# Attention into a mixture-of-depths layer: the hand-written order of 1162 items drawn anew

## The chip, the cores and the metric

The kernel runs on one core of a Trainium2 chip. The metric is device time in microseconds, from launch to end, the median of several runs. The engines of the core run side by side, each in its own order: PE (TensorE, matmuls), DVE (VectorE), ACT (ScalarE), POOL (GpSimd, which here mostly issues DMAs) and SP (SyncE, which only issues DMAs). An engine waits for another on semaphores.

## What is computed

Eight batches, twelve heads, 448 tokens, 64 columns per head. First attention with a squared ReLU, then for each batch a router picks 128 of the 448 tokens and a two-layer expert is added to them alone.

```python
scores = scale * np.matmul(q, k.transpose(0, 1, 3, 2))
attn = np.maximum(scores, 0.0) ** 2 / S
out = np.matmul(attn, v)                      # then heads side by side: x [8, 448, 768]

scores = np.einsum('bsd,d->bs', x, w_gate)
for b in range(B):
    top_idx = np.argpartition(-scores[b], capacity)[:capacity]      # capacity 128
    xe = x[b, top_idx]
    ye = np.maximum(xe @ w1, 0.0) @ w2                               # 768 -> 1024 -> 768
    g = 1.0 / (1.0 + np.exp(-scores[b, top_idx]))
    out[b, top_idx] = x[b, top_idx] + g[:, None] * ye
```

## The kernel before

The attention is cut into 24 units of four heads, three to a batch (unit u belongs to batch u // 3). For each unit, in the words of the order:

- `L,q,u`, `L,k,u`, `L,v,u` load the unit from memory (POOL's queue, cast to bf16 on the way). There are six buffers of each, so a load for unit u waits for the last reader of unit u - 6. Units 15 to 20 are loaded in two halves.
- `T,u,0` and `T,u,1` transpose q and k on PE (14 matmuls against an identity each, tile shape 128x64). `TE,u,2` copies both out of PSUM to `qkt` (DVE).
- `S,u,c` (c from 0 to 6) is a score block: four matmuls of tile shape 64x64 that run side by side. `R,u,c` is its ReLU, out of PSUM to `r_sb` (all on ACT). `Q,u,0,3` and `Q,u,3,7` square three and four of these blocks on DVE (`a_sb` from `r_sb`, twice the same input).
- `V,u,c` is the product with v (four 64x64 matmuls). `X,u` takes the unit's result out of PSUM to `xT_sb`, on ACT or DVE, as the letter A or D says.
- For units outside `BYDMA`'s batches `RT,u` transposes that back to rows on PE, and `RE,u` copies them to `x_rows`. For batches 5 and 6 `XB,u` does it with two transposing DMAs on SP's queue. `ST,b` stores a batch's rows (two DMAs on POOL's queue).

For each batch b the expert follows. `colx` and `colE` make the router's scores, `bt`, `rk`, `cs0`, `cs`, `rank` and `hots` rank the tokens, `sel,b` and `sE,b` give the 128 indices (`idx`, the last a reduction on DVE). `XG,b` gathers these rows from memory into `xg` (an indirect DMA on POOL's queue; it also needs the batch's `ST` to have landed). `XT,b` transposes them on PE, `xeE` copies them out, `gs` and `sig` make the sigmoid. `h,b,f` (f from 0 to 7) is the first layer, six matmuls of shape 128x128 each, `hE` its ReLU; `y,b,f` is the second layer, two matmuls of 384 columns, `yE` takes it to `gye` times the sigmoid, and `ADD,b` adds it to memory (an indirect DMA on POOL's queue). Batch 7, the last, takes its rows by matmuls (`xe`) instead of a gather. `W,i,part` loads parts of the weights. `PW,n,bank` are n matmuls on zeros that only keep PE busy at the start. `Zx`, `Zg`, `Zw` and the like are set-up: `Zh` copies the identity to fp32, `Zg` transposes the gate weights on PE, `Zc` makes constants.

A single string, ORDER, lists all these items, and a loop issues them as they stand. So it alone sets the order on every engine and queue: each engine takes its items in the string's order. The numbers at an item's end name a PSUM bank. There are eight banks, and an item that writes one waits for the last reader of what stood in it.

```python
with tc.manual_schedule():
    for item in ORDER.split():
        name, *args = item.split(",")
```

Transposes have a second form. A switch in their argument list does each in two halves of 64 columns, which gives them the tile shape 128x64 in place of 128x128:

```python
for h in HALF if by64 else (slice(0, 128),):
    nc.tensor.matmul(out=out_[h], lhsT=in_[:, h], rhs=ident, is_transpose=True,
                     skip_group_check=True, **flags)
```

Of the kernel before, what the change touches and what calls it, by code (L numbers as in the profile page):

```python
# [21 lines left out]
def kernel(  # L22
# [22 lines left out]
    BYDMA = (5,6)  # L45
# [60 lines left out]
    def L(what, u):  # L106
# [3 lines left out]
        if b not in BYDMA:  # L110
            nc.gpsimd.dma_start(out=dst, in_=src(t, u))  # L111
            return
# [224 lines left out]
    class Moe:  # L337
# [11 lines left out]

        def g(self, i, bank=None):  # L350
            if i == 0:
                self.at["g"] = bank
            nc.tensor.matmul(out=PS[:, self.at["g"], :S],
                             lhsT=wg_col[:, 1, i:i + 1].to_broadcast([128, 128]), rhs=self.xT[:, i].rearrange("p c n -> p (c n)")[:, :S],
                             start=(i == 0), stop=(i == NM - 1), skip_group_check=True)

        def colx(self, u, bank=None):
            if u == 0:
                self.at["col"] = bank
            for m in (2 * u, 2 * u + 1):  # L360
                for c in range(NR):
                    nc.tensor.matmul(out=PS[:, self.at["col"], c:c + 1], lhsT=self.xT[:, m, c, :],  # L362
                                     rhs=wg_col[:, 1 - (self.b in BYDMA), m:m + 1],
# [114 lines left out]
        def h(self, f, bank=None):  # L478
            if f == 0:
                self.at["h"] = bank  # L480
            bk, o = divmod(f * 128, 512)
            for m in range(NM):
                nc.tensor.matmul(out=PS[:, self.at["h"] + bk, o:o + 128],  # L483
                                 lhsT=w1_sb[:, m, f * 128:(f + 1) * 128], rhs=self.xeT[:, m, :],
                                 start=(m == 0), stop=(m == NM - 1), skip_group_check=True)
# [64 lines left out]
    R,7,2,A W,1,6,8 L,q,10 RT,3,0,1 rk,1,1 W,0,2,6 S,7,3,6 R,8,1,A RE,3,D rk,1,3 R,8,2,A Q,7,0,3 V,6,0,2 V,6,1  # L550
    V,6,2 W,0,3,6 L,k,11 R,7,3,A V,6,3 V,6,4 S,7,4,4 R,7,4,A S,7,5,0 T,10,0,6 T,10,1 XG,0 S,7,6,4 TE,10,2,D
    V,6,5 R,7,5,A R,7,6,A V,6,6 X,6,A cs0,1,0 cs,1,0 cs,1,1 cs,1,2 rank,1 hots,1 W,1,2,8 XT,0,0,1 S,8,3,4
    S,8,4,6 R,8,3,A R,8,4,A xeE,0,2,D sel,1,0 sE,1 S,8,5,2 W,0,1,6 h,0,0,0 h,0,1 h,0,2 R,8,5,A S,8,6,4 S,9,0,6
# [117 lines left out]
```

## Time and profile before

| | |
|---|---|
| runs, us | 198.83, 200.74, 202.49 (median 200.74) |
| the profiled execution, us | 199.68, of it the span 197.9 |
| mean granted TensorE clock | 0.987 |
| PE, DVE, ACT, POOL busy, us | 179.1, 164.7, 162.5, 109.2 |
| HBM traffic over the span | 284 GB/s |

The span runs from the first to the last instruction. What the launch takes beside it is 1.8 us. A busy share is an average over stages with different limits, so it says where to look and not what a change is worth; that is read in the stage itself, from what ends a wait there last.

### The profile page before, as it was taken

The numbers are of one execution on the slowest core, as the hardware profiler recorded it, in microseconds if no ns is written. First come the engines' busy times: TensorE is split into PE (matmuls) and PEld (weight loads), VectorE is DVE, ScalarE is ACT, GpSimd is POOL, SyncE is SP. The second block draws the span as 40 slices with busy tenths as digits, with TensorE's granted clock in tenths as the row PEclk, the third lists the DMA queues.
The fourth block names the chain that finished last, engine by engine and source line by source line (L and its number), as shares of the span: only waits on it lengthen the run. The fifth ranks groups of instructions, "written<-read, shape, count | busy, mean of one in ns | idle before, by whom it ended". The sixth has DMA issues, their size and how long they took to land.

```text
span 197.9 us, 7244 instructions
## 1 busy us (share of the span) xinstructions
PE 179.1 (91%) x3186; PEld 124.1 (63%) x3186; DVE 164.7 (83%) x234; ACT 162.5 (82%) x204; POOL 109.2 (55%) x160
## 2 busy tenths in 40 slices
PE   7778898989899999999998999999999999999900
PEld 7455455657567675875776767776676466688600
DVE  2489999999989999999999899999997999753310
ACT  4689999999999998999998999899998997242300
POOL 7968654641863967758897694460203140853360
PEclk9999999999999999999999999999999999999995
DMA  5999999999999999999999999999557892199291
GB/s 175 140 184 203 203 205 205 235 322 206 201 248 298 203 182 200 202 195 283 177 152 172 344 205 288 262 145 170 226 106 106 92 311 55 18 251 240 55 135 24
DMA packets 32333, 37.70 MB, mean 191 GB/s; under 512 B 8744, under 2 KB 29614, under 8 KB 31278
## 3 DMA queue, kind: packets, MB, share of 16 engines
q0 software_dynamic: 24928, 34.74, 91.1%
q1 hardware_dynamic: 7374, 2.50, 8.8%
q8 instruction: 25, 0.41, 0.8%
q14 instruction: 6, 0.05, 0.1%
HBM read 42.08 MB, written 14.16 MB: 284 GB/s over the span
## 4 chain that ended last, share of the span: by engine, by line
PE 56%; ACT 17%; DMA 11%; POOL 7%; issue 4%; DVE 2%; POOLq 0%; DVEq 0%
ACT r_sb L216 15%; PE ps L260 12%; PE ps L483 10%; PE ps L499 9%; PE ps L281 7%; PE ps L233 5%; DMA q_sb<-in_q_dram 4%; DMA v_sb<-in_v_dram 4%; PE ps L295 4%; POOL out_dram L517 3%; DMA xg<-out_dram,idx 3%; PE ps L209 2%; PE ps L374 2%; PE ps L362 2%; POOL k_sb L111 1%
## 5 line engine op out<-in xcount | busy, mean ns | idle before, releaser
L216 ACT ACTIVATE r_sb<-ps 128x896 bf16<-128x896 f32 x168 | 140.8, 955 | 8.1 <-PE ps L260 7.1
L274 DVE TENSOR_TENSOR a_sb<-r_sb 128x2688 bf16<-128x2688 bf16 (+1 forms) x48 | 84.9, 1785 | 2.4 <-ACT r_sb L216 2.0
L260 PE MATMUL ps<-qkt 64*64 64x448 bf16 x672 | 55.6, 362 | 4.3 <-ACT r_sb L216 2.5
L281 PE MATMUL ps<-a_sb,v_sb 64*64 64x448 bf16 x672 | 42.1, 351 | 0.8 <-ACT r_sb L216 0.8
L260 PEld LDWEIGHTS <-qkt 64*64 64x64 bf16 x672 | 21.4, 104 | 21.7 <-issue 11.4
L220 DVE COPY qkt<-ps 128x1792 bf16<-128x1792 bf16 (+3 forms) x26 | 26.1, 1006 | 4.4 <-PE ps L233 2.8
L281 PEld LDWEIGHTS <-v_sb 64*64 64x64 bf16 x672 | 21.5, 106 | 9.5 <-issue 2.2
L443 POOL DMA_INDIRECT xg<-out_dram,idx x7 | 12.2, 1748 | 27.4 <-DVE idx L427 23.6
L499 PE MATMUL ps<-w_sb,hT 128*128 128x384 bf16 x128 | 25.2, 326 | 0.0
L483 PE MATMUL ps<-xeT,w_sb 128*128 128x128 bf16 x384 | 24.5, 219 | 0.2 <-DVE xeT L220 0.2
L483 PEld LDWEIGHTS <-w_sb 128*128 128x128 bf16 x384 | 21.8, 98 | 4.5 <-issue 4.2
L517 POOL DMA_INDIRECT out_dram<-gye,idx x9 | 15.7, 1741 | 9.5 <-ACT g__3725 L476 5.9
L216 ACT ACTIVATE xT_sb<-ps 128x896 bf16<-128x896 f32 x16 | 15.4, 963 | 3.0 <-PE ps L281 2.9
L111 POOL DMA_DIRECT2D v_sb<-in_v_dram x18 | 13.2, 731 | 6.5 <-PE ps L281 2.8
L327 POOL DMA_DIRECT2D out_dram<-x_rows x8 | 4.5, 567 | 21.9 <-DMA x_rows<-xT_sb 13.6
L233 PEld LDWEIGHTS <-q_sb 128*64 128x64 bf16 x336 | 11.2, 111 | 6.5 <-issue 5.5
L233 PE MATMUL ps<-ident,q_sb 128*64 128x128 bf16 x336 | 14.1, 223 | 1.1 <-ACT r_sb L216 0.6
L499 PEld LDWEIGHTS <-hT 128*128 128x128 bf16 x128 | 10.6, 97 | 7.2 <-issue 2.2
L111 POOL DMA_DIRECT2D q_sb<-in_q_dram x17 | 12.7, 749 | 4.0 <-PE ps L233 1.5
L111 POOL DMA_DIRECT2D k_sb<-in_k_dram x17 | 12.5, 736 | 3.5 <-PE ps L260 1.5
L233 PE MATMUL ps<-ident,k_sb 128*64 128x128 bf16 x336 | 13.9, 220 | 0.0
L385 DVE SCALAR_TENSOR_TENSOR mask_sb<-ps,cols,tie 128x448 bf16<-128x448 f32 (+2 forms) x24 | 12.3, 546 | 0.7 <-PE ps L374 0.6
(123 smaller groups left out, 196.7 us busy)
## 6 DMA issues: line engine op xcount, KB each, us to landing
out_dram<-x_rows POOLq DMA_DIRECT2D x8, 768.0 KB
out_dram<-x_rows POOLq DMA_DIRECT2D x8, 576.0 KB, 7.3
v_sb<-in_v_dram POOLq DMA_DIRECT2D x18, 224.0 KB, 6.5
q_sb<-in_q_dram POOLq DMA_DIRECT2D x17, 224.0 KB
k_sb<-in_k_dram POOLq DMA_DIRECT2D x17, 224.0 KB, 8.3
w_sb<-in_moe_w_dram POOLq DMA_DIRECT2D x6, 256.0 KB
w_sb<-in_moe_w_dram POOLq DMA_DIRECT2D x8, 192.0 KB
k_sb<-in_k_dram POOLq DMA_DIRECT2D x12, 112.0 KB, 4.6
```

The source lines that it names most:

```text
L111: nc.gpsimd.dma_start(out=dst, in_=src(t, u))
L216: nc.scalar.activation(out=out_, in_=in_, func=func or AF.Copy, scale=scale)
L220: nc.vector.tensor_copy(out=out_, in_=in_)
L233: nc.tensor.matmul(out=PSB[HALF[j], at["T", u, w], n * 128:(n + 1) * 128], lhsT=s[:, j, c, :], rhs=ident, is_transpose=True, start=(n == 0 ...
L260: nc.tensor.matmul(out=PS[HALF[hf], bank + j, :S], lhsT=qkt[u][HALF[j], 1, c, hf, :], rhs=qkt[u][HALF[j], 0, :, hf, :], start=True, stop=True)
L274: nc.vector.tensor_tensor(out=a_sb[u][:, c0:c1], in0=r, in1=r, op=ALU.mult)
L281: nc.tensor.matmul(out=PS[HALF[j], at["V", u] + hf, :S], lhsT=v_sb[u % NBUF][HALF[hf], j, c, :], rhs=a_sb[u][HALF[hf], c, j, :], start=(c ...
L385: nc.vector.scalar_tensor_tensor(out=mask, in0=row[:, o:S], scalar=self.cols[:, c:c + 1], in1=tie[:, :S - o], op0=ALU.subtract, op1=ALU.is ...
L443: read = reads[self.b] = nc.gpsimd.indirect_dma_start(out=self.xg, out_offset=None, in_=out[0:self.b + 1].rearrange("b s d -> (b s) d"), i ...
L483: nc.tensor.matmul(out=PS[:, self.at["h"] + bk, o:o + 128], lhsT=w1_sb[:, m, f * 128:(f + 1) * 128], rhs=self.xeT[:, m, :], start=(m == 0) ...
L499: nc.tensor.matmul(out=PS[:, self.at["y"] + w, :384], lhsT=self.hT[:, f, :], rhs=w2_sb[:, f, w * 384:(w + 1) * 384], start=(f == 0), stop= ...
L517: add = nc.gpsimd.indirect_dma_start(out=out[0:self.b + 1].rearrange("b s (w d) -> (b s w) d", w=w), out_offset=bass.IndirectOffsetOnAxis( ...
```

## The change

The list of items that go by transposing DMAs now names units and no longer batches; it names the same six. Two items get a new argument: `h` and `y` can be done in halves of 64 columns, as transposes could. And the ORDER string is replaced by another of the same 1162 items.

```diff
-    BYDMA = (5,6)
+    BYDMA = (15,16,17,18,19,20)
...
-        if b not in BYDMA:
+        if u not in BYDMA:
...
+        def order(self, m):
+            return 1 - (NU * self.b + m // 2 in BYDMA)
...
-        def h(self, f, bank=None):
+        def h(self, f, by64, bank=None):
...
-        def y(self, f, part, bank=None):
+        def y(self, f, part, by64, bank=None):
             if bank is not None:
                 self.at["y"] = bank
             for w in ((0,), (1,), (0, 1))[part]:
-                nc.tensor.matmul(out=PS[:, self.at["y"] + w, :384], lhsT=self.hT[:, f, :],
-                                 rhs=w2_sb[:, f, w * 384:(w + 1) * 384], start=(f == 0),
-                                 stop=(f == NF - 1), skip_group_check=True)
+                for p in HALF if by64 else (slice(0, 128),):
+                    nc.tensor.matmul(out=PS[p, self.at["y"] + w, :384], lhsT=self.hT[:, f, p],
+                                     rhs=w2_sb[:, f, w * 384:(w + 1) * 384], start=(f == 0),
+                                     stop=(f == NF - 1), skip_group_check=True)
...
     ORDER = """
-    S,0,4,6 S,0,5,4 R,0,2,A R,0,3,A R,0,4,A R,0,5,A S,0,6,0 R,0,6,A Q,0,0,3 T,1,0,2 L,k,1 T,1,1 TE,1,2,D Lw Zg,4
-    Zw PW,15,5 S,1,0,0 S,1,1,2 R,1,0,A L,q,2 Q,0,3,7 L,k,2 T,2,0,4 T,2,1 S,1,2,6 S,1,3,0 R,1,1,A R,1,2,A R,1,3,A
...
+    Zx,1 R,0,2,A S,0,3,2 R,0,3,A Q,0,0,3 S,0,4,6 R,0,4,A S,0,5,4 S,0,6,0 R,0,5,A Zh T,1,0,2 T,1,1 TE,1,2,D
+    PW,19,6 S,1,0,2 T,2,0,4 R,0,6,A S,1,1,0 T,2,1 R,1,0,A R,1,1,A L,v,0 L,k,3 S,1,2,2 Zx,0 Q,0,3,7 V,0,0,6
```

The halves of `y` are asked for in five items (`y,1,0` to `y,1,2`, `y,4,6`, `y,4,7`), those of `h` in none. `RT` is done in halves in none (before: units 10 and 12), `XT` in batches 2, 3 and 5 (before: 3 alone). The engine letter differs in some evictions: `RE` of units 7, 9, 10, 22, 23, `X` of 9 and 20, `hE,7,1`, `xeE,1`, `xeE,7,1`, `yE,4`, `yE,7,0`, and the first two copies of `qkt`. `PW` has 62 matmuls before and 66 now.

Three places of the order follow. A name ends in a number that tells buffers apart; between the two kernels these numbers need not agree.

On DVE, at the start: the copy of unit 1's `qkt` with its neighbours, two squares (L274) of unit 0 and what stands between. Before:

```order
L274 TENSOR_TENSOR a_sb_283<-r_sb_237 128x2688
L220 COPY qkt_314<-ps_84 128x1792
L198 CAST wg_col_110<-ps_84 128x12
L274 TENSOR_TENSOR a_sb_283<-r_sb_237 128x3584
L220 COPY qkt_394<-ps_84 128x1792
L274 TENSOR_TENSOR a_sb_422<-r_sb_345 128x2688
```

The same place now:

```order
L274 TENSOR_TENSOR a_sb_271<-r_sb_261 128x2688
L187 CAST ident_f_119<-ident_118 128x128
L220 COPY qkt_316<-ps_84 128x1792
L274 TENSOR_TENSOR a_sb_271<-r_sb_261 128x3584
L220 COPY qkt_410<-ps_84 128x1792
L274 TENSOR_TENSOR a_sb_415<-r_sb_374 128x2688
```

The copy of the gate weights (`wg_col`) is gone from here, and the copy of the identity has come in ahead of `qkt`; it stood third on DVE before.

On POOL's queue, from batch 2's store (L327, L328) to batch 2's gather (`xg` with `idx`): loads of units 17 to 19, and one or two scatters (`gye`). Before:

```order
L327 DMA out_0_dram<-x_rows_1590 64x3072
L328 DMA out_0_dram<-x_rows_1590 64x2304
L115 DMA q_sb0_85<-in_q_dram 64x2x448 x2
L115 DMA q_sb4_89<-in_q_dram 64x2x448 x2
L517 DMA out_0_dram<-gye_2057,idx_1124 896x768
L115 DMA q_sb1_86<-in_q_dram 64x2x448 x2
L443 DMA xg_2339<-out_0_dram,idx_1580 128x768
L115 DMA v_sb0_97<-in_v_dram 64x2x448 x2
```

The same place now:

```order
L327 DMA out_0_dram<-x_rows_1612 64x3072
L328 DMA out_0_dram<-x_rows_1612 64x2304
L111 DMA v_sb1_98<-in_v_dram 128x2x448
L115 DMA q_sb5_90<-in_q_dram 64x2x448 x2
L115 DMA k_sb0_91<-in_k_dram 64x2x448 x2
L523 DMA out_0_dram<-gye_1694,idx_700 448x768
L115 DMA k_sb3_94<-in_k_dram 64x2x448 x2
L446 DMA xg_2237<-out_0_dram,idx_1591 128x768
L115 DMA q_sb3_88<-in_q_dram 64x2x448 x2
```

Between store and gather stands batch 0's scatter (448 rows down) where batch 1's stood (896), and behind the gather stands the q load of unit 15 (`q_sb3`) where the v load of unit 18 stood (`v_sb0`).

On DVE, around the reduction that gives batch 3's indices (`idx_2130` in both). Before:

```order
L274 TENSOR_TENSOR a_sb_2474<-r_sb_2357 128x2688
L220 COPY qkt_2534<-ps_84 128x1792
L427 TENSOR_REDUCE idx_2130<-ps_84 128x1
L220 COPY x_rows_2248<-ps_84 128x4x256
L368 TENSOR_TENSOR cols_2520<-ps_84,skew_106 128x4
L274 TENSOR_TENSOR a_sb_2474<-r_sb_2357 128x3584
```

The same place now:

```order
L220 COPY qkt_2557<-ps_84 128x1792
L371 TENSOR_TENSOR cols_2568<-ps_84,skew_106 128x4
L430 TENSOR_REDUCE idx_2130<-ps_84 128x1
L274 TENSOR_TENSOR a_sb_2487<-r_sb_2351 128x3584
L220 COPY x_rows_2182<-ps_84 128x4x256
```

A square now stands directly behind the reduction; before, a copy of rows and the scores of batch 4 stood between them.

## Rows read from the trace of the kernel before

**Rows 1.** The page, part 1: busy us, share of the span, instructions.

```profile
PE 179.1 (91%) x3186; PEld 124.1 (63%) x3186; DVE 164.7 (83%) x234; ACT 162.5 (82%) x204; POOL 109.2 (55%) x160
```

**Rows 2.** Windows: length, PE, PEld, DVE, ACT, POOL busy, clock, DMA share, GB/s.

```profile
13.00:51.00 38.00, 34.55 (x671) 21.79 (x668) 37.16 (x39) 36.78 (x46) 21.24 (x34) 1.00 1.22 223
51.00:188.00 137.00, 134.59 (x2382) 94.64 (x2378) 120.48 (x174) 117.28 (x148) 73.83 (x98) 1.00 0.99 192
```

**Rows 3.** Timeline, PE, 61 to 67 us: start, length, line, tile shape, count.

```profile
61.83 1.18 PE L483 MATMUL ps<-xeT,w_sb 128*128 128x128 bf16 x18
62.94 0.38 PE L260 MATMUL ps<-qkt 64*64 64x448 bf16 x4
63.26 0.84 PE L483 MATMUL ps<-xeT,w_sb 128*128 128x128 bf16 x12
64.03 0.38 PE L260 MATMUL ps<-qkt 64*64 64x448 bf16 x4
...
66.33 0.38 PE L260 MATMUL ps<-qkt 64*64 64x448 bf16 x4
66.52 0.38 PE L281 MATMUL ps<-a_sb,v_sb 64*64 64x448 bf16 x4
```

**Rows 4.** Timeline, all engines, 11 to 14 us; in brackets idle time before.

```profile
11.68 1.09 DVE L220 COPY qkt<-ps 128x1792 bf16<-128x1792 bf16 x1 [0.35 <-PE ps L233]
...
12.44 1.01 PE L209 MATMUL ps<-zero 128*128 128x128 bf16 x15
...
13.38 0.57 PE L260 MATMUL ps<-qkt 64*64 64x448 bf16 x8
...
13.82 0.92 ACT L216 ACTIVATE r_sb<-ps 128x896 bf16<-128x896 f32 x1 [0.85 <-PE ps L260]
```

**Rows 5.** Timeline, POOL, 88 to 100 us: store, scatter and gather among loads.

```profile
88.43 1.19 POOL L115 DMA_DIRECT2D k_sb<-in_k_dram  x2 [2.37 <-PE ps L281]
89.61 0.54 POOL L327 DMA_DIRECT2D out_dram<-x_rows  x1
...
90.69 2.40 POOL L115 DMA_DIRECT2D q_sb<-in_q_dram  x4
94.57 2.81 POOL L517 DMA_INDIRECT out_dram<-gye,idx  x1 [1.48 <-DVE gye L222]
...
98.99 1.61 POOL L443 DMA_INDIRECT xg<-out_dram,idx  x1 [0.30 <-issue]
```

**Rows 6.** Timeline, PE: unit 15's transposes (L233), gathers' (L295), a selection (L422).

```profile
101.29 0.56 PE L233 MATMUL ps<-ident,q_sb 128*64 128x128 bf16 x14
...
104.61 0.51 PE L295 MATMUL ps<-ident,xg 128*128 128x128 bf16 x6 [0.57 <-DMA xg<-out_dram,idx]
...
113.33 0.27 PE L422 MATMUL ps<-tok,hot__2129 128*128 128x2 bf16 x4
...
123.28 0.50 PE L295 MATMUL ps<-ident,xg 128*64 128x128 bf16 x12
```

**Rows 7.** Timeline, DVE and POOL: squares and gathers, 126 to 150 us.

```profile
126.82 1.55 DVE L274 TENSOR_TENSOR a_sb<-r_sb 128x2688 bf16<-128x2688 bf16 x1
...
128.36 2.02 DVE L274 TENSOR_TENSOR a_sb<-r_sb 128x3584 bf16<-128x3584 bf16 x1
128.72 2.54 POOL L443 DMA_INDIRECT xg<-out_dram,idx  x1 [2.79 <-DVE idx L427]
...
149.19 0.98 POOL L443 DMA_INDIRECT xg<-out_dram,idx  x1 [8.52 <-DVE idx L427]
```

**Rows 8.** Chain of work that ended last: start, length, what.

```profile
39.96 8.85 DMA q_sb<-in_q_dram
```

**Rows 9.** Timeline, PE and POOL, 185 us to the end.

```profile
185.38 1.62 PE L499 MATMUL ps<-w_sb,hT 128*128 128x384 bf16 x9
...
188.10 1.56 POOL L517 DMA_INDIRECT out_dram<-gye,idx  x1 [0.52 <-ACT gye L216]
...
189.96 1.55 POOL L517 DMA_INDIRECT out_dram<-gye,idx  x1 [0.26 <-issue]
```

More of the change, by code (lines that the diff above doesn't have):

```diff
@@ L353, in g @@
             nc.tensor.matmul(out=PS[:, self.at["g"], :S],
-                             lhsT=wg_col[:, 1, i:i + 1].to_broadcast([128, 128]), rhs=self.xT[:, i].rearrange("p c n -> p (c n)")[:, :S],
+                             lhsT=wg_col[:, self.order(i), i:i + 1].to_broadcast([128, 128]), rhs=self.xT[:, i].rearrange("p c n -> p (c n)")[:, :S],
                              start=(i == 0), stop=(i == NM - 1), skip_group_check=True)
@@ L362, in colx @@
                     nc.tensor.matmul(out=PS[:, self.at["col"], c:c + 1], lhsT=self.xT[:, m, c, :],
-                                     rhs=wg_col[:, 1 - (self.b in BYDMA), m:m + 1],
+                                     rhs=wg_col[:, self.order(m), m:m + 1],
                                      start=(m == 0 and c == 0),
@@ L482, in h @@
             for m in range(NM):
-                nc.tensor.matmul(out=PS[:, self.at["h"] + bk, o:o + 128],
-                                 lhsT=w1_sb[:, m, f * 128:(f + 1) * 128], rhs=self.xeT[:, m, :],
-                                 start=(m == 0), stop=(m == NM - 1), skip_group_check=True)
+                for p in HALF if by64 else (slice(0, 128),):
+                    nc.tensor.matmul(out=PS[p, self.at["h"] + bk, o:o + 128],
+                                     lhsT=w1_sb[:, m, f * 128 + p.start:f * 128 + p.stop],
+                                     rhs=self.xeT[:, m, :], start=(m == 0), stop=(m == NM - 1),
+                                     skip_group_check=True)
         def hE(self, part, eng):
@@ L550 @@
[L550 to L553, printed above, removed]
-    h,0,3 h,0,4 Q,7,3,7 h,0,5 S,9,1,2 h,0,6 Q,8,0,3 h,0,7 R,8,6,A S,9,2,4 R,9,0,A Q,8,3,7 V,7,0,6 V,7,1 L,v,8
@@ L610 @@
[L610 to L614 removed]
+    Zz LFq Cq,0 Zi Zs PW,32,0 LFk,0,2 Cq,1 Ck,0,2,D LFk,2,7 Zt Zm T,0,0,0 Zc L,q,1 TQE,0,4,D TK,0,2 TKE,0,2,D
@@ new lines @@
+    T,19,0,2 T,19,1 TE,19,2,D S,17,4,6 V,16,0,0 V,16,1 R,18,0,A V,16,2 S,17,5,4 L,v,18 hots,4 V,16,3 V,16,4
+    V,16,5 V,16,6 R,17,4,A R,17,5,A X,16,D XB,16 S,17,6,2 R,17,6,A h,3,0,0,6 sel,4,4 h,3,1,0 h,3,2,0 sE,4
+    S,18,1,0 S,18,2,2 S,18,3,4 h,3,3,0 h,3,4,0 h,3,5,0 h,3,6,0 h,3,7,0 R,18,1,A R,18,2,A R,18,3,A S,18,4,0
+    Q,17,0,3 XG,4 V,17,0,2 Q,17,3,7 V,17,1 R,18,4,A S,19,0,4 R,19,0,A V,17,2 V,17,3 V,17,4 V,17,5 hE,3,2,D
+    S,19,1,0 R,19,1,A V,17,6 X,17,D S,19,2,6 R,19,2,A T,20,0,4 T,20,1 TE,20,2,D S,18,5,0 XB,15 colx,5,0,2
@@ new lines @@
+    colx,5,1 colx,5,2 colE,5 R,18,5,A S,19,3,6 S,19,4,4 S,18,6,0 Q,18,0,3 R,19,3,A R,19,4,A R,18,6,A bt,5,2
+    gs,3,3 rk,5,2 rk,5,0 y,3,0,2,0,6 rk,5,3 y,3,1,2,0 y,3,2,2,0 sig,3 rk,5,1 y,3,3,2,0 y,3,4,2,0 S,19,5,0
+    S,19,6,4 Q,18,3,7 R,19,5,A cs0,5,3 XT,4,0,2 cs,5,0 R,19,6,A L,k,23 cs,5,1 cs,5,2 y,3,5,2,0 y,3,6,2,0
+    y,3,7,2,0 rank,5 yE,3,2,D xeE,4,2,A S,20,0,0 T,21,0,4 T,21,1 S,20,1,2 S,20,2,6 R,20,0,A R,20,1,A V,18,0,0
+    V,18,1 V,18,2 V,18,3 V,18,4 hots,5 TE,21,2,D V,18,5 L,v,21 S,20,3,2 S,20,4,4 V,18,6 R,20,2,A Q,19,0,3
@@ L615 @@
+    y,7,6,1,0 y,7,7,1,0 sel,7,3 sig,7 yE,7,1,A sE,7 ADD,6 y,7,1,0,0 y,7,2,0,0 y,7,3,0,0 y,7,4,0,0 y,7,5,0,0
+    y,7,6,0,0 y,7,7,0,0 yE,7,0,A ADD,7,1 ADD,7,0
     """
```

152 lines of the change are left out of this document (74 added, 78 removed).

## The prediction

> **What bounds the kernel now.** I read the page's busy shares first: TensorE (PE) is busy 91% of the span, and VectorE (DVE) and ScalarE (ACT) stand close behind at 83% and 82% [rows 1]. With three engines so near each other the mean says little, so I read the stages. The table of windows has two [rows 2]. From 13 to 51 us DVE works 37.16 and ACT 36.78 of 38 us, and PE idles 3.45: the evictions set the pace. From 51 to 188 us PE works 134.59 of 137 us, so it idles 2.4 us, while ACT has 19.7 us to spare and DVE 16.5: PE sets the pace, to the last matmul. The granted clock is 1.00 in both, the 2.4 GHz level. Behind the last matmul (188.2 us) come two scatters from POOL, the last issued at 189.96 [rows 9], and the span ends at 197.9: a tail of 9.7 us. So only three things can move the time: ACT's start and its holes before 51 us, PE's own work and holes after it, and the tail.
>
> I then went through PE's rows one piece of the order at a time. A piece of the same kind always takes the same time from its start to the next start, except where the shape of the tile in use changes. The four matmuls of a score block are followed after 0.19 us by value matmuls of the same 64x64 shape (66.33 to 66.52), but after 0.32 us by 128x128 matmuls (62.94 to 63.26): that change costs 0.13. The other way, 18 matmuls of the expert's first layer take 1.11 us up to a score block (61.83 to 62.94) and 12 take 0.77 (63.26 to 64.03), so six take 0.34 and the change of shape 0.10 [rows 3]. I take 0.11 for a change in either direction. Where I speak of PE work between two places below, it is the sum of such pieces over the order, waits left out.
>
> **The change, part by part.** The code of the two new arguments and of the renamed list computes what it did: the same six units (15 to 20) go by transposing DMAs. What is left is the order, and the few engine letters and halvings in it.
>
> *Changes of shape.* I counted them in the two orders: 154 before, 138 after. Eleven of the 16 lie before the last score block of unit 9 (about 67 us), five behind it. Those five are safe gain, as PE alone sets the pace there: 5 times 0.11 is 0.6 us. The other eleven (1.2 us) lie mostly where ACT and DVE set the pace, and I count them at nothing: their cover is the 3.45 us that PE idles there, and if that cover were gone they would be worth up to 1.2 more. Term: -0.6, between 0 and -1.8.
>
> *Halved matmuls.* Five second-layer pieces are now done in column halves, ten matmuls becoming 20, to match a neighbour of the 128x64 shape; the transposes of x_rows lose their halves (two pieces), the gathered rows gain them (two more). Batch 3's gathered rows, turned in 12 halves, take PE 0.50 us (123.28), batch 2's in 6 whole ones 0.51 (104.61) [rows 6]: no price. For 384 columns no row exists. If the halves did not run side by side, ten more matmuls at 0.18 (nine take 1.62 in the tail [rows 9]) would cost 1.8. The transposes are the nearest rows, so 0; the bounds are 0 and +1.8.
>
> *The start.* In the old order PE runs two transposes of the gate weights and 15 idle-filling matmuls (12.44 to 13.38) before unit 1's first scores, though DVE's copy of qkt, on which these wait, ends at 12.77. ACT therefore idles 0.85 us before 13.82 [rows 4]. Now the gate transposes come some units later, and 19 fillers stand straight behind unit 1's transposes; these end near 11.4, and 19 at the rows' 0.06 us end near 12.6. The scores can begin at 12.8, 0.6 us sooner. DVE's copy of the identity, now ahead of that qkt copy, has the 0.35 us of DVE idle there for cover. As ACT and DVE are continuously busy from here to 51 us, what ACT gains here carries on. Term: -0.6; bounds 0 (a load or DVE holds it instead) and -0.85 (all of ACT's idle).
>
> *Engine letters.* DVE gives ACT one x_rows eviction, one of hT, two of xeT and two of gye on balance and takes two of xT. At 0.8 to 0.9 us each that is about +3.4 us for ACT and as much less for DVE. Nearly all lie behind 51 us, where ACT's 19.7 us of slack covers them; without it they would cost the 3.4.
>
> *Batch 2's gather* (xg). It is the one PE hole of note behind 51 us: PE waits 0.57 us at 104.61 [rows 6]. It was issued late, at 98.99, behind batch 1's scatter, which had itself waited 1.48 for DVE [rows 5]. The new order puts batch 0's scatter there, whose data are long ready, and the selection that the gather needs stands 17.5 us of PE work ahead of its transposes, where it stood 12.3. I take the hole away: -0.6, bounds 0 and -0.6 (what comes late instead is under the rivals).
>
> *Batch 3's gather.* Its selection and its transposes (113.33 and 123.28 [rows 6]) stood 9.8 us of PE work apart; now it is 7.9, four unit transposes and a score block fewer. Needed: 0.6 for the selection and DVE's reduction, some 0.5 until POOL issues, the issue itself and its landing. An issue takes 0.98 us at the least (149.19) and 2.54 where a square of DVE runs beside it (128.72 beside 128.36) [rows 7]. Batch 2's gather landed 4.0 us after its issue's end (98.99 plus 1.61, to 104.61). In the new order a square stands right behind the reduction, so 0.6 + 0.5 + 2.54 + 4.0 = 7.6 of 7.9: just covered. Price 0; +1 us if the landing takes a quarter longer.
>
> A page of the Trainium skill says why, SBUF — State Buffer, section Who interferes with whom: a VectorE instruction with two SBUF inputs and a GpSimd instruction that reads SBUF cannot run together, whoever came first keeps the port. The trace agrees: the square ends at 130.38, and 0.98 behind it gives 131.36 against the measured 131.26 [rows 7]. By this rule a gather behind whose reduction two squares follow each other could wait through both, and the time would come out as in the second rival.
>
> *Loads.* The 70 loads, 14 weight parts and eight stores are the same in number and size, only in other places on POOL's queue. A load at the busiest time takes 8.85 us [rows 8]. Going by the places, each load now has at least the lead that the closest ones of before lived with, except unit 15's (below). I charge nothing; the cover is that lead.
>
> *The tail.* The same four scatters stand at the end with the same waits; the last one still follows its predecessor at 1.86 us (188.10 to 189.96) [rows 9]. 0.
>
> Sum: -0.6 - 0.6 - 0.6 = -1.8 us, from the profiled execution's 199.68 to 197.9. That execution lies 1.06 under the median of the three runs (200.74), so I go half of that up: **198.4**.
>
> **The rivals.**
> *Nothing comes of it* (199.7 to 200.7): every 0.1 us saved turns into a wait for ACT, as the two orders give ACT and DVE the same work up to unit 9's last eviction. For it: ACT and DVE above 96% busy from 13 to 51 us. Against it: PE is not waiting behind 51.
> *Gathers held by squares* (199.9 to 202): behind batch 1's and batch 4's reductions two squares now follow each other (1.55 and 2.02 us [rows 7]); a gather held through both is issued 3.6 us later. Its transposes stand 11 us of PE work behind the selection. Needed then: 0.6 and 0.5, 3.6 and 0.98, 4.0, together 9.7, and 13.6 if issue and landing take the 8.85 of a load at the busiest time. So 0 to 2.5 us stand uncovered for each of the two and 0 to 1 for batch 3's: 2 to 4 us in the middle of that, on the 197.9. Against it: batch 4's gather had one square beside it before, and PE did not wait for it. It is the page's rule at its worst.
> *Unit 15 late* (slower: 204): its q load now stands right behind batch 2's gather on POOL; before, unit 18's v stood there, which is needed much later. From batch 2's store to this load POOL has 11.5 us to issue: 1.1 for the store, 0.6 for each of ten half loads, 2.81 for a scatter, 1.61 for the gather [rows 5]; then 5.6 (batch 2's gather) to 8.85 us to land. If the store goes out at 89.61 as before, the load lands between 106 and 109, and PE, which keeps its order, stands at unit 15's transposes from 99.5 (101.29 before [rows 6], less the 1.8): 7 to 10 us. But the store's rows are ready about 4 us of PE work sooner, POOL's 2.37 us of wait ahead of it are gone and so are the scatter's 1.48 [rows 5], which leaves 0 to 2. It decides from a stall of 5.8 us (4.0 net of the gains).
> *All holes close* (195.5): ACT's 1.2 us of idle before 51 and PE's 2.4 behind it go, with the 0.6: -4.2. For it: the selections of batches 2, 4 and 6 stand further ahead of their gathers' use (batch 6's 9.2 us of PE work, before 6.8), and eleven changes of shape fewer let PE run ahead before 67 us. Against it: PE's 2.4 us behind 51 us are many small holes, and the one of 0.57 is the largest I know of.
>
> **How the numbers follow.** The forecast has 0.45, with a range of its own from 197.2 to 200.2 (half of all its terms' bounds to either side). Nothing comes of it 0.17, gathers held 0.12, unit 15 late 0.10, all holes close 0.16. Two per cent, about what a measurement tells from no change here (the three runs spread by that), is 4.0 us. Faster by more needs all holes closed: 0.16, that whole case. Slower by more is unit 15 late and the upper end of the held gathers: 0.12. Within: 0.72. The range leaves out the far halves of the two outer cases: 196.0 to 202.0.
>
> **What would show it.** In the profile after: PE's holes between 10 and 14 us, and ACT's idle before unit 1's first eviction (0.85 now, near 0.25 if I am right); the windows from 51 us on with PE busy time about 0.6 less for the same work; no PE wait for xg near 100 us, and one under 1 us near 121; unit 15's transposes near 99.5 without a wait; the last scatter 1.9 us behind its predecessor. I am wrong if PE shows a wait for a DMA above 1 us, if ACT's idle before 51 us grows, or if the halved second-layer pieces take 0.5 us instead of 0.33.

## The result: 1.2% faster, 197.69 us

The changed kernel takes 197.69 us (median of 4 runs, 197.13 to 198.28), the kernel before 200.01 us beside it (198.83 to 202.49): a ratio of 0.9884, with a 95% interval from 0.9838 to 0.9929. The forecast was 198.4 us, by a sum of -1.8 us on the profiled execution. The profiled execution of the changed kernel took 198.28 us, 1.4 us less than that of before, with a span of 196.6 us. Both kernels were run again later side by side on another chip: 0.9911 (0.9881 to 0.9941). Before's own median differs from chip to chip (198.95 to 200.55 us in the three later groups), so only ratios within a group are compared, and traces of different groups with care.

The page's busy line (to set beside [rows 1]) and the table of windows (as [rows 2]: length, busy time of PE, PEld, DVE, ACT and POOL, clock, DMA share, GB/s) of the changed kernel:

```profile
PE 178.5 (91%) x3196; PEld 124.9 (64%) x3196; DVE 162.2 (83%) x230; ACT 164.2 (84%) x208; POOL 109.6 (56%) x159
```

```profile
13.00:51.00 38.00, 33.94 (x667) 22.44 (x663) 37.25 (x42) 37.82 (x47) 20.74 (x34) 1.00 1.22 223
51.00:188.00 137.00, 133.75 (x2383) 93.91 (x2379) 118.74 (x169) 118.09 (x151) 74.98 (x98) 1.00 1.06 193
```

The shares of the page have hardly moved and would explain nothing. The windows do: from 13 to 51 us ACT now idles 0.18 us where it idled 1.22. Its last matmul ends at 186.98 us, before at 188.24.

The start, a timeline of all engines (to set beside [rows 4]):

```profile
10.91 0.58 PE L233 MATMUL ps<-ident,k_sb 128*64 128x128 bf16 x14
11.17 0.22 DVE L187 CAST ident_f<-ident 128x128 f32<-128x128 bf16 x1
11.42 1.24 PE L209 MATMUL ps<-zero 128*128 128x128 bf16 x19
11.60 1.09 DVE L220 COPY qkt<-ps 128x1792 bf16<-128x1792 bf16 x1 [0.22 <-PE ps L233]
...
12.75 0.38 PE L260 MATMUL ps<-qkt 64*64 64x448 bf16 x4
...
13.18 0.92 ACT L216 ACTIVATE r_sb<-ps 128x896 bf16<-128x896 f32 x1 [0.29 <-PE ps L260]
```

The scores of unit 1 begin at 12.75 instead of 13.38, and ACT idles 0.29 in place of 0.85. Batch 2's and batch 3's gathered rows and unit 15's transposes, a timeline of PE (to set beside [rows 6]; no row has a bracket, so PE waited for nothing):

```profile
100.11 0.53 PE L295 MATMUL ps<-ident,xg 128*64 128x128 bf16 x12
100.47 0.56 PE L233 MATMUL ps<-ident,q_sb 128*64 128x128 bf16 x14
...
121.61 0.53 PE L295 MATMUL ps<-ident,xg 128*64 128x128 bf16 x12
```

Two holes are new, both put down to nothing that the profile shows ("issue"), 1.13 us together:

```profile
138.14 0.32 PE L505 MATMUL ps<-w_sb,hT 128*128 128x384 bf16 x1 [0.53 <-issue]
...
152.49 0.38 PE L260 MATMUL ps<-qkt 64*64 64x448 bf16 x4 [0.60 <-issue]
```

The second ends as DVE's copy of unit 22's qkt does (152.44). The tail is what it was: the last scatter follows its predecessor by 1.86 us [rows 9].

```profile
186.84 1.56 POOL L523 DMA_INDIRECT out_dram<-gye,idx  x1 [0.85 <-ACT gye L216]
...
188.70 1.56 POOL L523 DMA_INDIRECT out_dram<-gye,idx  x1 [0.26 <-issue]
```

### The profile page after: what moved, and what is told of

It reads as the page before. It is cut to its first block, busy times and chain, and to the rows that moved or that the text cites. A ratio compares the mean times of both kernels' runs of the same rounds, so it can differ in the third digit from the quotient of the medians.

```text
span 196.6 us, 7271 instructions
## 1 busy us (share of the span) xinstructions
PE 178.5 (91%) x3196; PEld 124.9 (64%) x3196; DVE 162.2 (83%) x230; ACT 164.2 (84%) x208; POOL 109.6 (56%) x159
## 4 chain that ended last, share of the span: by engine, by line
PE 56%; ACT 30%; issue 6%; DVE 3%; POOL 2%; ACTq 0%; DVEq 0%; POOLq 0%
ACT r_sb L216 26%; PE ps L260 12%; PE ps L487 10%; PE ps L505 10%; PE ps L281 9%; PE ps L233 5%; PE ps L295 3%; ACT xT_sb L216 2%; PE ps L365 2%; PE ps L209 2%; DVE a_sb L274 2%; POOL out_dram L523 2%; PE ps L377 1%; DVE qkt L220 1%; PE ps L438 1%
## 5 line engine op out<-in xcount | busy, mean ns | idle before, releaser
L274 DVE TENSOR_TENSOR a_sb<-r_sb 128x2688 bf16<-128x2688 bf16 (+1 forms) x48 | 85.0, 1784 | 2.1 <-ACT r_sb L216 2.0
L281 PE MATMUL ps<-a_sb,v_sb 64*64 64x448 bf16 x672 | 41.6, 350 | 0.0
L260 PEld LDWEIGHTS <-qkt 64*64 64x64 bf16 x672 | 22.3, 104 | 22.3 <-issue 12.0
L281 PEld LDWEIGHTS <-v_sb 64*64 64x64 bf16 x672 | 20.8, 106 | 8.4 <-issue 0.5
L487 PE MATMUL ps<-xeT,w_sb 128*128 128x128 bf16 x384 | 25.2, 219 | 0.0
L505 PE MATMUL ps<-w_sb,hT 128*128 128x384 bf16 (+1 forms) x138 | 24.2, 326 | 0.5 <-issue 0.5
L523 POOL DMA_INDIRECT out_dram<-gye,idx x9 | 18.0, 2003 | 8.1 <-ACT gye L216 6.0
L327 POOL DMA_DIRECT2D out_dram<-x_rows x8 | 4.4, 550 | 30.2 <-DMA x_rows<-xT_sb 16.9
L446 POOL DMA_INDIRECT xg<-out_dram,idx x7 | 11.0, 1565 | 18.0 <-DVE hT L218 8.7
L505 PEld LDWEIGHTS <-hT 128*128 128x128 bf16 (+1 forms) x138 | 11.5, 99 | 8.3 <-issue 2.6
L233 PE MATMUL ps<-ident,q_sb 128*64 128x128 bf16 x336 | 14.3, 225 | 1.8 <-ACT r_sb L216 1.6
L233 PEld LDWEIGHTS <-q_sb 128*64 128x64 bf16 x336 | 11.4, 112 | 6.4 <-issue 5.6
L233 PE MATMUL ps<-ident,k_sb 128*64 128x128 bf16 x336 | 14.0, 221 | 0.0
L216 ACT ACTIVATE xT_sb<-ps 128x896 bf16<-128x896 f32 x14 | 13.5, 967 | 0.6 <-PE ps L281 0.6
L220 DVE COPY x_rows<-ps 128x1024 bf16<-128x1024 bf16 x15 | 10.3, 687 | 2.9 <-PE ps L295 2.8
```

Source lines behind the costliest of these rows:

```text
L216: nc.scalar.activation(out=out_, in_=in_, func=func or AF.Copy, scale=scale)
L220: nc.vector.tensor_copy(out=out_, in_=in_)
L233: nc.tensor.matmul(out=PSB[HALF[j], at["T", u, w], n * 128:(n + 1) * 128], lhsT=s[:, j, c, :], rhs=ident, is_transpose=True, start=(n == 0 ...
L260: nc.tensor.matmul(out=PS[HALF[hf], bank + j, :S], lhsT=qkt[u][HALF[j], 1, c, hf, :], rhs=qkt[u][HALF[j], 0, :, hf, :], start=True, stop=True)
L274: nc.vector.tensor_tensor(out=a_sb[u][:, c0:c1], in0=r, in1=r, op=ALU.mult)
L281: nc.tensor.matmul(out=PS[HALF[j], at["V", u] + hf, :S], lhsT=v_sb[u % NBUF][HALF[hf], j, c, :], rhs=a_sb[u][HALF[hf], c, j, :], start=(c ...
```

## The experiments

Three groups of four, each group on one chip. The theory is the prediction's: the start, the changes of shape behind 67 us and batch 2's wait are worth about 0.6 us each and add. Against it: that one of them is the whole gain, that ACT's gain is eaten behind, or that the gain is something else.

**Only the start, old order.** The gate transposes with their loads and copy moved away, 19 fillers for 15:

```
- T,1,1 TE,1,2,D Lw Zg,4 Zw PW,15,5 S,1,0,0 ... X,1,D RT,1,0,4
+ T,1,1 TE,1,2,D PW,19,5 S,1,0,0 ... X,1,D Lw Zg,4 Zw RT,1,0,4
```

> The order of before, with only the start of after: the two gate transposes, their loads and their copy moved from ahead of unit 1's first scores to ahead of x_rows' first transposes, 19 fillers there in place of 15. If the start is a term of its own that carries through the stage set by the evictions: ACT idles near 0.25 us before unit 1's first eviction (0.85 before), every later milestone and the last matmul come 0.5 to 0.6 us sooner (188.24 to about 187.7), ratio 0.997. If a load or DVE holds the stage instead (the rival): the idle shrinks but comes back before unit 9's last eviction, last matmul unchanged, ratio 1.000. If the whole gain of after came from the start: ratio 0.988.

Measured: 1.0028 (1.0000 to 1.0056). Nothing was gained, and the timelines of PE and ACT say why:

```profile
11.37 0.58 PE L233 MATMUL ps<-ident,k_sb 128*64 128x128 bf16 x14
12.61 1.22 PE L209 MATMUL ps<-zero 128*128 128x128 bf16 x19 [0.65 <-ACT r_sb L216]
13.76 0.38 PE L260 MATMUL ps<-qkt 64*64 64x448 bf16 x4
```

```profile
14.19 0.92 ACT L216 ACTIVATE r_sb<-ps 128x896 bf16<-128x896 f32 x1 [0.83 <-PE ps L260]
```

The fillers stand at 12.61 though the transposes ahead end at 11.95: PE waits 0.65 us for ACT. They write bank 5, which ACT is still evicting for unit 0. In before the gate transposes wait just so in bank 4. The edit left this wait in place, and as much work behind it: 1.15 us from the fillers to the scores (12.61 to 13.76), where the gate transposes and 15 fillers took 1.16 (12.22 to 13.38). So it was not the gate transposes that made the start late; whether it was the wait or the length of the work, this run cannot tell.

**Only batch 2's gather, old order.** The scatters of batches 0 and 1 exchanged:

```
- RT,11,0,0 ADD,1 colx,3,0,1 ... rk,4,0 ADD,0 y,2,2,2
+ RT,11,0,0 ADD,0 colx,3,0,1 ... rk,4,0 ADD,1 y,2,2,2
```

> The order of before with batch 0's and batch 1's scatters exchanged on POOL, so that batch 2's gather stands behind the one whose rows are long ready. If the wait was only the scatter's: POOL's 1.48 us of wait ahead of that gather is gone, PE's wait for xg at 104.6 too, the last matmul comes 0.57 us sooner, ratio 0.997. If the hole is only moved (the rival that nothing comes of a PE hole, as evictions or another wait take it): xg arrives in time but the last matmul is where it was, ratio 1.000.

Measured: 1.0003 (0.9973 to 1.0032). In the timeline of PE the wait is gone, but the matmuls come no sooner than in before (104.61 [rows 6]):

```profile
101.89 0.56 PE L233 MATMUL ps<-ident,q_sb 128*64 128x128 bf16 x14
...
104.50 0.49 PE L295 MATMUL ps<-ident,xg 128*128 128x128 bf16 x6
```

Unit 15's transposes stand at 101.89, 0.60 later than in before (101.29 [rows 6]): small holes at 95 to 100 us took what the wait gave. The last matmul ended at 187.62, 0.62 sooner than in the first profile of before and 0.10 later than in the second (below). What made the small holes stays open.

**Both of these edits together.**

> The order of before with both edits: the start of after and the two scatters exchanged. If the terms add: last matmul 1.1 to 1.2 us sooner (near 187.1), which is nearly the whole of what after gained, ratio 0.994 (197.69 of 200.01 would be 0.988). If changes of shape are the larger part of the gain: 0.4 us or less sooner than before, or at any rate less than half of after's 1.26 us.

Measured: 0.9999 (0.9969 to 1.0029). As the start edit did nothing, this is the exchange alone once more, with the same answer. In the timeline of PE no wait is left for batch 2's rows, but one stands at batch 3's, where before had none [rows 6]:

```profile
124.29 0.53 PE L295 MATMUL ps<-ident,xg 128*64 128x128 bf16 x12 [0.46 <-DMA xg<-out_dram,idx]
```

The run says nothing on whether the terms add.

**The start put back in the new order.**

```
- T,1,1 TE,1,2,D PW,19,6 S,1,0,2 ... X,1,D Lw Zg,4 Zw S,2,6,0
+ T,1,1 TE,1,2,D Lw Zg,4 Zw PW,15,6 S,1,0,2 ... X,1,D S,2,6,0
```

> The order of after, with only its start put back as before (gate transposes and 15 fillers ahead of unit 1's first scores). If the start carries: ACT idles near 0.85 us there, unit 9's last eviction and the last matmul come 0.5 to 0.6 us later than in after (186.98 to about 187.5), ratio against before 0.991 to 0.992. If after's first stage hides it: the same times as after, 0.988.

Measured: 0.9958 (0.9926 to 0.9991). It costs half of the gain or more, but the profiled execution cannot size the term, since something else happened in it. Windows, then PE's timeline:

```profile
12.00:14.00 2.00, 1.74 (x17) 1.72 (x17) 1.84 (x3) 1.02 (x2) 1.65 (x3) 0.62 1.23 195
14.00:16.00 2.00, 2.00 (x25) 0.99 (x23) 1.07 (x1) 0.92 (x1) 2.00 (x3) 0.52 1.27 204
```

```profile
12.26 0.29 PE L192 MATMUL ps<-ident_f,wg 6*128 6x6 f32 x2 [0.65 <-ACT r_sb L216]
12.49 1.78 PE L209 MATMUL ps<-zero 128*128 128x128 bf16 x15
```

The granted clock (eighth column) is 0.62 and 0.52, the 1.2 GHz level for most of these four microseconds, and the 15 fillers take 1.78 us where they took 1.01 [rows 4]. PE had idled 0.65 just ahead, but so it had in before, at a clock of 1.00. The other executions have no trace, but their mean clock is on record: in six of the twelve it was 0.980 or less, and these took 199.69 to 202.56 us; in the other six it was 0.983 to 0.986, and these took 198.18 to 199.66. So part of what this run lost seems to have gone with the clock.

**Only the banks, old order.** So the next run left everything where it stood and changed two digits (the expectation below says three):

```
- Lw Zg,4 Zw PW,15,5 S,1,0,0
+ Lw Zg,6 Zw PW,15,7 S,1,0,0
```

> The order of before, with three digits changed: the gate transposes write bank 6 and the 15 fillers bank 7, where they wrote 4 and 5. In before, and in the run that only moved the gate transposes away, PE idles 0.65 us ahead of this place for ACT's eviction of banks 4 and 5; banks 6 and 7 are free one eviction earlier. If the start's gain comes from the bank and not from what stands there: no PE idle of 0.65 at 11.6 us, ACT idle near 0.25 before unit 1's first eviction (0.85 before), unit 9's last score block and the last matmul 0.5 to 0.6 us sooner than in the profile of before, a granted clock of 1.00 there, and a ratio of 0.993 to 0.997 (the lower end if executions of before lose clock there, as the run with the old start in the new order did). If the start gives nothing (the rival): 1.000.

Measured: 0.9998 (0.9974 to 1.0022). In the trace the start does what was expected, nearly (a timeline of PE, then of ACT):

```profile
11.59 1.01 PE L209 MATMUL ps<-zero 128*128 128x128 bf16 x15
...
12.90 0.57 PE L260 MATMUL ps<-qkt 64*64 64x448 bf16 x8 [0.30 <-ACT r_sb L216]
```

```profile
13.33 0.92 ACT L216 ACTIVATE r_sb<-ps 128x896 bf16<-128x896 f32 x1 [0.48 <-PE ps L260]
```

The 0.65 is gone, and 0.30 stands in its place: the first scores go into bank 0, which ACT evicts last of unit 0; the new order puts them into bank 2. So with the same work in place other banks took ACT's idle from 0.85 to 0.48, where after has 0.29; that bank 2 for the first scores makes up the rest is read from this row and was not run. Yet the time shows nothing, and the interval leaves out the 0.993 to 0.997 that was expected, if barely. Against the second profile of before (below; on another chip) unit 9's last eviction ends 0.66 us sooner (68.51 for 69.17), but the last matmul, at 187.15, only 0.37. Most of the difference goes in one place (timeline of PE):

```profile
123.13 0.38 PE L260 MATMUL ps<-qkt 64*64 64x448 bf16 x4 [0.28 <-ACT xT_sb L216]
```

And the span is 197.1 us, 10.0 us behind the last matmul (9.6 and 9.5 in the two profiles of before): the last scatter took longer to land. The 0.37 us would be 0.2%, which the interval does not rule out.

**The new order without its 19 fillers.**

```
- T,1,1 TE,1,2,D PW,19,6 S,1,0,2
+ T,1,1 TE,1,2,D S,1,0,2
```

> The order of after without the 19 idle-filling matmuls between unit 1's transposes and its first scores. They compute nothing. If they hold TensorE's clock: PE idles 1.2 us at 11.5, the granted clock behind it falls to the 1.2 GHz level for some us (0.62 and 0.52 in the stretches from 12 to 16 us, as the run with the old start in the new order showed), and the time is 1 to 1.6 us longer than after's: ratio against before 0.993 to 0.997. If they are idle work and the fall in that run had another cause: clock 1.00 and the time of after, 0.988.

Measured: 0.9902 (0.9868 to 0.9935), the changed kernel's time within the interval. PE idles 1.26 us at 11.5, and the profile has a clock of 1.00 in every stretch from 0 to 188 us. So the second case of the expectation came true: the fillers are not what kept the clock in that execution. Over whole executions the mean granted clock ran from 0.971 to 0.989 in its twelve runs and from 0.985 to 0.988 in the changed kernel's first four, but from 0.973 to 0.988 in twelve later ones, so the runs don't show that fillers matter. This profile has neither of the two "issue" holes of after's first one, and its last matmul ends at 185.37.

**Twelve extra fillers early, and late, in the new order.** One filler ahead of each of 12 score blocks whose predecessor has the 64x64 shape, in the same bank: two changes of shape each.

```
- S,3,2,0        (early, units 1 to 5)     S,15,4,2        (late, units 10 to 20)
+ PW,1,0 S,3,2,0                           PW,1,2 S,15,4,2
```

> The order of after with one idle-filling matmul put in at 12 places between 64x64 pieces of units 1 to 5 (15 to 38 us), each into the bank that the next score block writes: 24 more changes of the tile's shape. By the prediction ACT and DVE set the pace there, so that the cover holds: each place costs PE 0.29 (two changes at 0.11 and 0.06 of work), 3.4 us in all, of which unit 9's last score block and the end show 0 to 0.8. If PE sets the pace there too: 3.4 us later, ratio against before near 1.005.

> The order of after with the same 12 idle-filling matmuls between 64x64 pieces of units 10 to 20 (70 to 145 us): 24 more changes of shape. If PE alone sets the pace there and a change costs 0.11: the last matmul 3.4 us later than in after (3.0 to 3.5, as small holes take a little), ratio against before near 1.005. If a change of shape costs nothing of itself: 0.8 us, ratio 0.992. If ACT or DVE set the pace there: 0, ratio 0.988.

Measured: early 0.9949 (0.9919 to 0.9979), late 1.0019 (0.9986 to 1.0052), where the changed kernel has 0.9884 and 0.9911. A place in the late one, timeline of PE:

```profile
107.38 0.38 PE L260 MATMUL ps<-qkt 64*64 64x448 bf16 x4
107.70 0.23 PE L209 MATMUL ps<-zero 128*128 128x128 bf16 x1
107.86 0.38 PE L260 MATMUL ps<-qkt 64*64 64x448 bf16 x4
```

From block to block it is now 0.48 us, where neighbours of one shape stand 0.19 apart [rows 3]: 0.29 more, of which 0.06 is the filler, so 0.11 for each change. That is the price that the prediction read from the old trace. Windows (columns as above) of the late run from unit 9's last eviction to the last matmul, then of the early run from unit 1's first eviction to unit 9's last:

```profile
68.58:188.52 119.94, 119.48 (x2082) 82.87 (x2076) 101.77 (x146) 100.62 (x128) 64.09 (x81) 1.00 0.99 185
12.93:69.21 56.28, 52.80 (x992) 33.14 (x992) 54.19 (x65) 55.74 (x70) 31.84 (x50) 1.00 1.20 226
```

Beside the second profile of the changed kernel (shown with the crossed orders below) the late twelve add 2.56 us to PE's busy time (119.48 for 116.92), and the last matmul ends 2.57 later (188.52 for 185.95), with unit 9's last eviction at 68.58 in both. So all that PE took more comes out at the end. It is less than the 3.4 that twelve times 0.29 would be, because at three of the twelve places the two blocks stood 0.29 to 0.34 us apart without a filler too. The early twelve add 2.30 us (52.80 for 50.50), and the window is 1.0 longer (56.28 us for 55.28). The cover held for a little over half of it.

The early run lost another 1.33 us far behind, at batch 5's gathered rows. Timelines of PE and POOL:

```profile
157.97 0.41 PE L295 MATMUL ps<-ident,xg 128*64 128x128 bf16 x8 [1.33 <-DMA xg<-out_dram,idx]
```

```profile
144.50 0.56 POOL L327 DMA_DIRECT2D out_dram<-x_rows  x1 [12.14 <-DMA x_rows<-xT_sb]
...
145.92 1.70 POOL L523 DMA_INDIRECT out_dram<-gye,idx  x1 [0.30 <-issue]
...
152.75 1.61 POOL L446 DMA_INDIRECT xg<-out_dram,idx  x1 [5.08 <-DVE cols L371]
```

Batch 5 is the first whose units go by transposing DMAs. Its store waits 12.14 us for them, and its gather reads what the store wrote. In the second profile of the changed kernel the same three stand 3.4 to 4.4 us sooner, and PE does not wait:

```profile
141.14 0.56 POOL L327 DMA_DIRECT2D out_dram<-x_rows  x1 [9.45 <-DMA x_rows<-xT_sb]
...
142.56 2.92 POOL L523 DMA_INDIRECT out_dram<-gye,idx  x1 [0.30 <-issue]
...
148.40 1.03 POOL L446 DMA_INDIRECT xg<-out_dram,idx  x1 [2.88 <-DMA out_dram<-x_rows]
```

**Before and after once more, and the two orders crossed.** The last group asks in which part the gain lies. Up to unit 9's last eviction (69 us) both orders have done nearly the same pieces, so each first part can be followed by the other's rest:

```
old_new: before ... S,9,6,6 R,9,6,A | Zx,2 gs,0,4 sig,0 L,q,14 T,11,0,2 ... after
new_old: after  ... S,9,6,6 W,1,2,8 R,9,6,A | W,1,0,8 T,11,0,2 ... before
```

> The kernel before, unchanged, profiled on the chip of the three runs below. If what the first profile showed is a property of the order: ACT idles 0.85 us before unit 1's first eviction, PE waits for xg at 104.6 (0.5 to 0.9 us) and idles 0.4 to 0.6 us at unit 8's first scores (50.8), ratio 1.000. A hole that is not there again belonged to that execution alone.

> The changed kernel, unchanged, profiled again. PE's holes of 0.53 us at 137.6 and 0.60 us at 151.9 in the first profile did not show in two of the three runs that have the same order there. If they belonged to that execution: they are gone or smaller, the last matmul ends near 185.9 instead of 186.98, and the ratio stays 0.984 to 0.993. If they belong to the order: they are there again.

> The order of before up to unit 9's last eviction (about 67 us), then the order of after for all that is left. Unit 9's last score block as in before (67.3); from there to the last matmul 119.3 to 120.3 us, as after has it, in place of 120.8. If both parts of the order gain, as the rows say (five changes of shape and the wait for xg behind 67 us, 0.6 each; the start before it): ratio 0.993 to 0.995. If the whole gain comes from behind 67 us: 0.988. If it comes from before 67 us: 1.000.

> The order of after up to unit 9's last eviction, then the order of before. Unit 9's last score block 0.8 to 1.0 us sooner than in before (66.4), the rest as in before with PE's wait for xg, last matmul 0.8 to 1.0 sooner. If both parts gain: ratio 0.994 to 0.996. If the whole gain comes from the part before 67 us: 0.988. If what is gained there goes into waits behind it, as in the run that only changed the banks: 1.000.

Measured: before again 0.9995 (0.9960 to 1.0029), after again 0.9911 (0.9881 to 0.9941), old then new 0.9993 (0.9963 to 1.0022), new then old 0.9962 (0.9933 to 0.9992).

The two profiles on one chip are the cleanest comparison there is. Windows cut at two events of each kernel, the start of unit 1's first eviction and the end of unit 9's last, up to the last matmul (before again, then after again; columns as above):

```profile
13.98:69.17 55.19, 51.22 (x976) 33.38 (x974) 53.80 (x64) 55.19 (x69) 32.61 (x51) 1.00 1.20 229
69.17:187.52 118.35, 117.14 (x2065) 82.73 (x2060) 102.72 (x149) 98.47 (x125) 61.63 (x81) 1.00 0.97 186
```

```profile
13.30:68.58 55.28, 50.50 (x980) 33.68 (x980) 53.99 (x65) 55.28 (x70) 31.59 (x49) 1.00 1.21 229
68.58:185.95 117.37, 116.92 (x2070) 82.77 (x2064) 101.55 (x146) 99.92 (x128) 64.81 (x81) 1.00 1.02 188
```

In the first window ACT is busy 55.19 of 55.19 and 55.28 of 55.28 us: it never stops, and the new order, which takes 0.09 more, computes one gate value (`sig,0`) more there. So 0.68 us gained at 13.98 arrive as 0.59 at 69.17. Behind it PE is the bound: the new order needs 0.98 us less, of which 0.76 is PE idle (1.21 against 0.45). Together 1.57 us at the last matmul, 1.6 in the span.

Of before's first profile one thing was not there again: ACT's 0.40 us of idle at 50.78. It showed in four of the seven profiles that have the old first part and not in the other three. Of the two "issue" holes of after's first profile, the one at 137.6 is in none of the six other profiles of the new rest; near 152 us two others show idle time, put down to DVE there, of 0.26 us in the second profile of the changed kernel and 0.76 in two pieces with the old start put back. They are more the execution's than the order's.

The run of new then old shows one way in which a single term gets lost. PE's timeline there and in before again:

```profile
104.09 0.51 PE L295 MATMUL ps<-ident,xg 128*128 128x128 bf16 x6 [1.27 <-DMA xg<-out_dram,idx]
```

```profile
104.54 0.51 PE L295 MATMUL ps<-ident,xg 128*128 128x128 bf16 x6 [0.85 <-DMA xg<-out_dram,idx]
```

Its first part ends 0.86 us sooner than before's (68.31 against 69.17), but batch 2's gathered rows come only 0.45 sooner: the wait grew by 0.42. So half of this gain was lost in that gather, with the old rest behind it. It is not a rule: in the run that only changed banks PE came 0.66 us sooner too, and the same wait is 0.83 us, no longer than in before again. There the loss came later, at 123.13.

Old then new has an artefact of the seam: the gate values of batch 0, moved behind the seam, write bank 4 while DVE still copies unit 8's result out of it.

```profile
68.75 0.29 PE L474 MATMUL ps<-wg_col,xeT 128*128 128x1 bf16 x6 [1.32 <-DVE xT_sb L222]
```

Without these 1.32 us its median (198.95) would be near 197.6, a ratio of about 0.993, which is what was expected of it; that is arithmetic and was not run. Its profile, from which the 1.32 comes too, is of the longest of its twelve executions (201.90), so nothing more is read from it. By that estimate the first part gives about 0.4% and the rest about 0.7%, and against the 0.9 and 1.2% measured for the whole change the two parts would add, within what these intervals can tell. As measured they give 0.4 and 0.1% and stay short of it, so that the parts add is not shown.

## Why the prediction was right, point by point

*What bounds it.* Right in both halves, but the border lies at 68.6 us and not at 51: from 13.3 to 68.6 us ACT sets the pace, without a break, and PE behind that.

*Changes of shape.* The price of 0.11 us was right, and so was the split: the traces count 154 changes and 138, five of the difference behind the cut. But the -0.6 for these five is not there in full. PE's busy time behind the cut falls by 0.22 us (117.14 to 116.92; 117.35 to 117.01, 0.34, in the first pair of profiles). About 0.16 of that is the six matmuls of batch 0's gate value, which the new order does ahead of the cut, and the halved pairs below cost about 0.1. So 0.2 to 0.3 us is what the changes of shape can have given there; where the rest stayed is open. Before 67 us ACT's unbroken work covers the eleven: the new order saves 0.72 us of PE work in that window (51.22 to 50.50) and ACT takes 0.09 longer. The cover is not thick, as the early fillers showed.

*Halved matmuls.* 0, right. By lines and shapes, changed kernel:

```profile
L505 PE MATMUL ps<-w_sb,hT 128*128 128x384 bf16 x118 | 22.2, 326 | 0.5 <-issue 0.5
...
L505 PE MATMUL ps<-w_sb,hT 128*64 128x384 bf16 x20 | 2.0, 328 | 0.0
```

Twenty halves keep PE busy 2.0 us, 0.10 each; 118 whole ones 22.2, 0.19 each. The halves run side by side, and ten pairs cost 0.1 us more than ten whole ones.

*The start.* -0.6 was right in size: 0.68 at the first eviction, 0.59 where PE takes over. The step behind it was wrong, and that the size came out is luck. The prediction blamed the gate transposes and the fillers that stand there; taking the transposes away gained nothing. The old trace has a row that says so, ahead of both:

```profile
12.22 0.29 PE L192 MATMUL ps<-ident_f,wg 6*128 6x6 f32 x2 [0.65 <-ACT r_sb L216]
```

PE idles there for ACT. What counts is the bank: 4 and 5 are evicted one step after 6 and 7, and 0 after those. The new order changed banks and pieces together, so the size was that of the banks.

*Engine letters.* 0, right: behind unit 9 ACT works 1.45 us more and DVE 1.17 less, and ACT still idles 17 us there. The forecast had 3.4 us for either engine; over the whole span it is 1.7 more for ACT and 2.5 less for DVE.

*Batch 2's gather.* No wait in any profile of the new rest, so the -0.6 is there, and more: in the five profiles that have the old rest with its old scatters the wait is 0.57 to 1.27 us. What the prediction did not say is that this term and the start need not add, as new then old shows. In the old order the exchange alone and the banks alone each came to nothing in time, and their traces show small holes and later waits in place of the gain. The two were not put into the old order together, so it is not shown that they reach the end only together.

*Batch 3's gather.* "Just covered" was right: no wait in either profile of the changed kernel, 0.16 us in the run without fillers.

*Loads and tail.* 0 and 0, right. But the new rest has a cover that the prediction did not price: batch 5's store hangs on transposing DMAs. When these are late, PE waits for its gather: 1.33 us with the early fillers and 1.11 in old then new.

*The sum.* -1.8 forecast, -1.6 between the two profiles on one chip, -1.4 between the first two, in which a hole of 0.4 in before and two of 1.13 in after belonged to the executions. The start gave -0.6 for -0.6, what lies behind 67 us -1.0 for -1.2. Of this -1.0, 0.76 is PE's idle and 0.22 its work, where the forecast had 0.6 for the wait and 0.6 for the changes of shape: the total came out because one term was too small and the other too large. The medians moved by 2.3 us, more than the profiles; the interval, 1.4 to 3.2 us, does not tell the two apart.

*The rivals.* Nothing comes of it: fell for the whole change, but it is what the time showed for each edit of the old order. Unit 15 late: its transposes stand at 100.47 without a wait. All holes close: ACT's do, but PE still idles 0.45 us behind 68.6 us in the better profile, and the time is 1.6 to 2.2 us above the 195.5. Gathers held by squares: batch 1's gather in the second profile of the changed kernel, between the two squares (timelines of DVE and POOL):

```profile
61.21 1.55 DVE L274 TENSOR_TENSOR a_sb<-r_sb 128x2688 bf16<-128x2688 bf16 x1
...
62.67 2.02 DVE L274 TENSOR_TENSOR a_sb<-r_sb 128x3584 bf16<-128x3584 bf16 x1
```

```profile
61.74 1.90 POOL L446 DMA_INDIRECT xg<-out_dram,idx  x1 [2.25 <-DVE idx L430]
```

Its issue takes 1.90 us, ends at 63.64, 0.9 behind the first square, and is over while the second still runs, which at 2.02 us is no longer than elsewhere [rows 7]. Batch 4's is alike (126.23, 2.06 us). So the gather is held by one square and not by two: its issue takes 1.90 and 2.06 us, where the rival's sum had 4.6 (3.6 and 0.98). The Trainium skill (SBUF — State Buffer, section Who interferes with whom) calls the shared port an exclusive lock; the trace agrees for the first square, but the last 0.9 us of the issue run beside the second, which is not slowed, so the two are not kept apart for the whole of both.

## What to carry to other kernels

When an engine waits ahead of a piece of filling or moved work, look at the bank that the work writes before you blame the work: two digits took away here a wait of 0.65 us that moving the pieces had left. Do not expect terms that lie ahead of the same DMA to add: of 0.86 us gained ahead of batch 2's gather in one run, 0.42 went into a longer wait for it, though in another run 0.66 us passed it whole. A gain of half a microsecond can be lost further on, in another wait or in the landing of the last DMA, so follow it through the trace to the end before you call an edit worthless. Before you explain a hole of half a microsecond, profile the same kernel a second time: of the four of 0.4 to 0.6 us that the first two profiles showed, only the wait for batch 2's rows was there again in full.

## What was not expected of the hardware

The granted clock fell to the 1.2 GHz level for about 3.4 us (an estimate from 0.62 and 0.52 in two stretches of 2 us) in one profile of fourteen, behind 0.65 us of PE idle; the same idle in six other profiles, and 1.26 us of it in one, left the clock at 1.00. What decides it stays open.

The transposing DMAs of batch 5 released its store at 141.1 us in the second profile of the changed kernel and at 144.5 in the run with the early fillers, 3.4 us apart, though PE was only 0.7 us later there (batch 4's gathered rows at 136.49 and 137.17).
